# Transposes of q and k by DMA, and the four products with v of a pair of heads in one go, in an attention and MLP kernel

## The chip, the cores and the metric

The kernel runs on one core of one Trainium2 chip. The metric is the time of one execution on the device in microseconds (us). Three runs of the kernel before gave a median of 1263.84 us (1262.47 to 1264.2). All durations below come from one more execution, which the hardware profiler recorded.

## What is computed

```python
# q, k, v: (8 batches, 12 heads, 448 rows, 64); w_in 768x2048; w_out 2048x768
scores = q @ k.transpose(0, 1, 3, 2) / sqrt(64) - log(448)
attn = 1 / (1 + exp(-scores))          # a sigmoid, no softmax
x = (attn @ v).transpose(0, 2, 1, 3).reshape(8 * 448, 768)
h = x @ w_in
out = (h - tanh(h)) @ w_out
```

## The kernel before

**Numbers in two halves.** From batch 2 on, a float32 matrix is kept as two float16 parts, a high half and a low half (what the high half leaves over), after it was multiplied by a power of two, and a product is three float16 matmuls: high by high, high by low, low by high. Batch 0 multiplies float32 throughout its attention; batch 1 has its scores in halves and its products with v in float32.

**The engines.** TensorE (PE) multiplies into PSUM; ScalarE (ACT) and VectorE (DVE) read PSUM and SBUF; GpSimd (POOL) only adds squares; SyncE (SP) issues the DMAs, in order. The order of PE, ACT, DVE and POOL is the order in which the program records its instructions; SP's order is left to the scheduler.

**A batch.** `moe1` (line 663) multiplies x by w_in, 288 matmuls with no attention between them; ACT and DVE make `h - tanh(h)` of it (`mix`, line 740) and split it into halves. `moe2` (line 772) multiplies by w_out: 48 steps of six matmuls (`po`) for three full row tiles, then 16 steps for the remaining 64 rows (`por`), which count half. Between these steps `second` (line 939) runs blocks of the attention of the *next* batch, at the steps listed in `BLOCKS` (8, 12, ... 52).

**A block.** `stream` (line 429) yields them. A pair of heads, g, has four chunks of 112 rows of k and so two blocks, i = 0 and i = 1, of two chunks each. In program order a block records:

- transposes on PE: k of pair g+2 if i = 1 (with a small matmul behind it in the same PSUM tile, which spreads the sums of squares for the scales, line 316), q of pair g+1 if i = 0. Four transposes of 112x128 each (line 299) fill a PSUM tile with the tag `tr`, of which there is one;
- the scores of the two chunks (line 362: 12 matmuls, `sc`), each chunk's sigmoid on ACT (line 371, `a`);
- between the two sigmoids, the halves K of pair g+2 or Q of pair g+1 (`parts`, line 332): high half on ACT (Q) or DVE (K), low half on DVE (line 340);
- `do_av`: the products with v (line 386, `acc`, 12 matmuls) of the two chunks of the *block before*; after the fourth chunk ACT evacuates x and squares it;
- the halves of v of pair g+1 (i = 0, line 348), the halves of this block's weights (`ahl`, lines 377 and 378), the loads of pair g+3 (i = 0) or the norms of pair g+3 on ACT (i = 1, line 308).

Temporary tiles of `mix`, the sigmoids and `ahl` share eight buffers (`TP`). K and Q have two buffers each.

**The end of a batch.** The block at index `ALONE` of `BLOCKS` finishes the batch's last products with v; three steps later `batch_scales` (line 608) takes the largest sum of squares and makes the halves `xhl` (lines 625 and 626) for the next `moe1`, in three portions, two steps apart. The blocks behind it already belong to the batch after. The first blocks of all run in the first batch, in `moe1_32` and `first`, beside the conversion of w_out.

Of the kernel before, what the change touches and what calls it, by code (L numbers as in the profile page):

```python
# [8 lines left out]
F16 = mybir.dt.float16  # L9
BF16 = mybir.dt.bfloat16  # L10
F32 = mybir.dt.float32
# [3 lines left out]
AF = mybir.ActivationFunctionType  # L15
ALU = mybir.AluOpType
# [3 lines left out]
P = 128  # L20
D = 64
CK = 112
# [12 lines left out]
class Builder:  # L35
# [6 lines left out]

    BLOCKS = (8, 12, 16, 20, 24, 28, 32, 36, 40, 44, 48, 52)
    TAIL = (1, 2, 3, 4, 5)
    ALONE = 8
    BLOCKS0 = (2, 5, 8, 12, 16, 20, 24, 31, 38)
    BLOCKS1 = (4, 7, 10, 13, 16, 19, 22, 25, 28, 32, 36, 40, 44, 48, 52)

    TP = 8
    SHIFT = 4  # L50

    def __init__(self, ctx, tc, q, k, v, w_in, w_out, out):
        self.tc, self.nc = tc, tc.nc
# [29 lines left out]
        self.wo = self.wp.tile([P, self.NF * 2 + self.SHIFT, 2, self.HALF], F16, name="wo")  # L83

    def warm(self, n):

# [25 lines left out]

    def where(self, kind, r, i=0):

        t, n, m = (self.wi, self.NB, 256) if kind == "in" else (self.wo, 1, self.HALF)
        f = t.rearrange("p a b c -> p (a b c)").bitcast(F32)
        r = r * n + i * self.NF + self.SHIFT
        return f[:, r * m : (r + n) * m]

    def conv_load(self, p):  # L120
# [88 lines left out]

    def split(self, t, n, S, act):  # L210

        F = t[:, n + self.SHIFT].rearrange("p b c -> p (b c)").bitcast(F32)
# [81 lines left out]
    def transpose(self, n, name, tag="tr", bufs=1, t=None):  # L294
        nc = self.nc
        if t is None:
            t = self.ps.tile([P, 512], F32, name=name, tag=tag, bufs=bufs)
        for c in range(4):
            nc.tensor.transpose(t[:, c * CK : (c + 1) * CK], n[:, c].rearrange("p h d -> p (h d)"), self.ident[:CK, :CK])  # L299
        return t[:, : self.S]  # L300
# [7 lines left out]
            self.nc.scalar.activation(junk, t.rearrange("p a b d -> p (a b d)"), AF.Square, accum_out=ss[:, i : i + 1])  # L308
        return ss[:, :n]

    def scales(self, ss, pb):

        nc = self.nc
        n = ss.shape[1]
        pb = pb[:, self.S : self.S + n]
        nc.tensor.matmul(pb, self.onesf[:CK, :], ss, start=True, stop=True)
        t = self.sm.tile([P, 3], F32, name="tn")
        nc.scalar.activation(t[:, :n], pb, AF.Relu, bias=self.tiny, scale=2.1)
        y = self.pow2(t[:, :n], n, "n")
        i = self.sm.tile([P, 3], F32, name="in")  # L320
        nc.vector.tensor_scalar(i[:, :n], y, 2.0**49, None, op0=ALU.mult)
        s = self.sm.tile([P, 3], F32, name="sn", bufs=3)
        nc.vector.reciprocal(s[:, :n], i[:, :n])
        r = self.sm.tile([P, 2], F32, name="rn", bufs=5)
        nc.vector.scalar_tensor_tensor(
            r[:, 0:1], i[:, 0:1], 1.0 / math.sqrt(D), i[:, 1:2], op0=ALU.mult, op1=ALU.mult
        )
        if n == 3:
            nc.vector.tensor_scalar(r[:, 1:2], y[:, 2:3], 2.0**49 / A_SCALE, None, op0=ALU.mult)
        return s, r  # L330

    def parts(self, t, s, name, act):

        nc = self.nc
        o = self.qk.tile([P, 2, self.S], F16, name=name, tag=name)
        if act:
            nc.scalar.activation(o[:, 0], t, AF.Copy, scale=s)  # L337
        else:
            nc.vector.tensor_scalar(o[:, 0], t, s, None, op0=ALU.mult)
        nc.vector.scalar_tensor_tensor(o[:, 1], t, s, o[:, 0], op0=ALU.mult, op1=ALU.subtract)  # L340
        return o

    def prep_v(self, vn, s):
# [85 lines left out]
    def stream(self):  # L429
# [5 lines left out]
        G = (self.B - 1) * NP  # L435
        at = lambda g: (1 + g // NP, g % NP)
        splits = lambda g: at(g)[0] >= self.AV32
        qk, v, ss, sc, K, Q, vv = {}, {}, {}, {}, {}, {}, {}
# [8 lines left out]
            if g < G:  # L447
                ss[g] = self.norms(qk[g] + ([v[g]] if splits(g) else []))

        def turn(g, n, name):  # L450
            return self.transpose(qk[g][n], name) if g < G else None

        def turn_k(g):
            if g >= G:
                return None
            t = self.ps.tile([P, 512], F32, name="kT", tag="tr", bufs=1)
            turned = self.transpose(qk[g][0], "kT", t=t)
            sc[g] = self.scales(ss.pop(g), t)
            return turned

        def parts_k(g, t):
            if g < G:
                K[g] = self.parts(t, sc[g][0][:, 0:1], "K", not splits(g) and g not in (2, 3))

        def parts_q(g, t):
            if g < G:
                Q[g] = self.parts(t, sc[g][0][:, 1:2], "Q", True)
                qk.pop(g)

        def prep_v(g):  # L470
# [11 lines left out]
        norms(1)  # L482
        yield 0, False
        for g in range(2):
            parts_k(g, turn_k(g))
            yield 450, False
            parts_q(g, turn(g, 1, "qT"))
            load(g + 2)
            yield 450, False
        norms(2)  # L490
# [16 lines left out]

        for g in range(G):
            for i in range(2):
                if i:  # L510
                    t = turn_k(g + 2)
                elif g:
                    t = turn(g + 1, 1, "qT")
                pss = [self.scores(c, K[g], Q[g]) for c in (2 * i, 2 * i + 1)]
                aa = [self.weigh(pss[0], sc[g][1][:CK, 0:1])]
                if i:
                    parts_k(g + 2, t)
                elif g:
                    parts_q(g + 1, t)
                aa.append(self.weigh(pss[1], sc[g][1][:CK, 0:1]))  # L520
                do_av()
                if i == 0:
                    if g == 0:
                        prep_v(0)
                    prep_v(g + 1)
                if splits(g):
                    aa = [self.split_a(a) for a in aa]
                todo.extend((g, 2 * i + n, a) for n, a in enumerate(aa))
                if g and i == 0:
                    load(g + 3)  # L530
                elif g:
                    norms(g + 3)
                yield 2750, True
# [350 lines left out]
    def first(self, rest):  # L884
# [33 lines left out]
    def batch(self, b):  # L918
# [70 lines left out]
```

## Time and profile before

| | us |
|---|---|
| median of three runs | 1263.84 |
| the profiled execution's own time | 1264.8 |
| its span, first to last instruction | 1262.5 |
| PE busy | 1235.0 |
| DVE busy | 946.7 |
| ACT busy | 940.2 |
| POOL busy | 38.6 |

In a profile "busy" is time with an instruction in work; matmuls follow one another in a pipeline, so a group's busy time divided by its count is less than the mean duration of one. A wait is put down to the instruction that came last before the waiting one could go. "Landing" is the time from the issue of a DMA to its completion. A tile's name stands without its buffer number.

### The profile page before, as it was taken

To read this page: it belongs to the slowest core of one execution; us is meant where nothing else is said; L and a number is where in the kernel's file an instruction comes from. 1 tells how busy PE (TensorE), PEld (TensorE's weight loads), DVE (VectorE), ACT (ScalarE), POOL (GpSimd) and SP (SyncE) were. 2 spreads that over 40 slices of the span, in tenths; PEclk is the share of its full clock that TensorE was granted. 3 is DMA by queue.
4 is the path that set the end of the run, shared out by engine and by line. 5 is a ranking of instruction groups with operands and counts; after the bars stand their busy time and mean duration, and the time that the engine had idled before them with its cause. 6 is when DMAs were issued, how large, how long until landed. Compare 5 with 4: busy or idle time off the path is not lost.

```text
span 1262.5 us, 20449 instructions
## 1 busy us (share of the span) xinstructions
PE 1235.0 (98%) x8011; PEld 685.3 (54%) x8011; DVE 946.7 (75%) x1473; ACT 940.2 (74%) x1325; POOL 38.6 (3%) x38
## 2 busy tenths in 40 slices
PE   9889889999999999999999999999999999999998
PEld 3245445555556555665555655555556655555555
DVE  5989988789876797676965798667976769645930
ACT  6957788958998688886878688886888868753820
POOL 0100000000010000100000000000000000000000
PEclk9999999999999999999999999999999999999999
DMA  9943254100122101220022200221012200100001
GB/s 261 299 126 90 56 162 136 49 20 1 36 73 57 42 2 42 65 65 7 1 58 64 56 1 16 64 58 41 1 43 67 62 7 1 28 14 20 1 13 32
DMA packets 114367, 70.52 MB, mean 56 GB/s; under 512 B 91872, under 2 KB 104416, under 8 KB 114272
## 3 DMA queue, kind: packets, MB, share of 16 engines
q1 hardware_dynamic: 113344, 69.00, 20.6%
q8 instruction: 63, 1.03, 0.3%
q10 hardware_dynamic: 928, 0.23, 0.1%
q14 instruction: 32, 0.26, 0.1%
HBM read 58.20 MB, written 11.01 MB: 55 GB/s over the span
## 4 chain that ended last, share of the span: by engine, by line
PE 74%; DVE 14%; ACT 6%; issue 3%; DMA 3%; SPq 0%; DVEq 0%; ACTq 0%
PE ph L676 30%; PE po L798 25%; PE sc L362 6%; PE acc L386 5%; PE por L836 3%; DVE ahl L378 2%; ACT a L371 2%; DVE xhl L626 2%; DMA raw<-moe_w_in 1%; PE acc L396 1%; PE qT L299 1%; DVE xhl L625 1%; ACT wo L214 1%; DVE stb L151 1%; DVE m L750 1%
## 5 line engine op out<-in xcount | busy, mean ns | idle before, releaser
L798 PE MATMUL po<-wo,g 128*128 128x384 f16 x2304 | 391.4, 326 | 1.0 <-ACT o L827 1.0
L676 PE MATMUL ph<-xhl,wi 128*128 128x448 f16 x2016 | 382.6, 352 | 0.0
L798 PEld LDWEIGHTS <-g 128*128 128x128 f16 x2304 | 219.5, 98 | 171.3 <-issue 30.4
L676 PEld LDWEIGHTS <-wi 128*128 128x128 f16 x2016 | 196.7, 98 | 185.0 <-issue 1.8
L371 ACT ACTIVATE a<-sc,nls,rn 112x896 f32<-112x896 f32 x168 | 179.9, 1095 | 45.4 <-PE sc L362 38.3
L378 DVE SCALAR_TENSOR_TENSOR ahl<-a,ahl 112x896 f16<-112x896 f32 x144 | 155.7, 1122 | 58.6 <-ACT ahl L377 57.9
L746 ACT ACTIVATE u<-ph,ih 128x896 f32<-128x896 f32 x64 | 64.4, 1006 | 98.9 <-PE ph L676 95.3
L377 ACT ACTIVATE ahl<-a 112x896 f16<-112x896 f32 x144 | 128.0, 939 | 0.0
L362 PE MATMUL sc<-Q,K 64*112 64x448 f16 x1008 | 116.1, 362 | 3.8 <-ACT a L371 2.8
L750 DVE SCALAR_TENSOR_TENSOR m<-ph,ihk,u 128x896 f32<-128x896 f32 x64 | 73.5, 1148 | 54.9 <-ACT th L748 54.6
L386 PE MATMUL acc<-ahl,vhl 112*64 112x448 f16 x864 | 96.4, 357 | 0.5
L660 ACT ACTIVATE g<-m,Sg 128x896 f16<-128x896 f32 x64 | 66.6, 1041 | 34.1 <-DVE m L764 28.7
L764 DVE COPY_PREDICATED m<-u,th 128x896 f32<-128x896 uint32 x64 | 77.3, 1207 | 6.9 <-DVE m L761 0.5
L661 DVE SCALAR_TENSOR_TENSOR g<-m,Sg,g 128x896 f16<-128x896 f32 x64 | 73.4, 1147 | 8.8 <-ACT g L660 8.8
L340 DVE SCALAR_TENSOR_TENSOR Q<-qT,sn,Q 128x448 f16<-128x448 f32 x42 | 28.6, 682 | 67.9 <-ACT Q L337 67.9
L362 PEld LDWEIGHTS <-K 64*112 64x112 f16 x1008 | 60.6, 128 | 32.5 <-issue 6.8
L761 DVE SCALAR_TENSOR_TENSOR m<-q,m 128x896 f32<-128x896 f32 x64 | 69.9, 1093 | 8.3 <-ACT q L760 0.9
L706 PE MATMUL ph<-x,wi 128*128 128x448 f32 x192 | 74.8, 539 | 0.0
L751 DVE SCALAR_TENSOR_TENSOR th<-ph,ih,th 128x896 f32<-128x896 f32 x64 | 73.3, 1145 | 0.0
L763 ACT ACTIVATE u<-u,b 128x896 f32<-128x896 f32 x64 | 66.7, 1043 | 5.6 <-DVE m L750 3.6
L757 DVE SCALAR_TENSOR_TENSOR m<-q,m 128x896 f32<-128x896 f32 x64 | 69.5, 1087 | 0.0
L386 PEld LDWEIGHTS <-vhl 112*64 112x64 f16 x864 | 43.5, 109 | 47.8 <-issue 26.1
(134 smaller groups left out, 1323.0 us busy)
## 6 DMA issues: line engine op xcount, KB each, us to landing
raw<-moe_w_in SPq DMA_DIRECT2D x24, 512.0 KB, 7.5
rawo<-moe_w_out SPq DMA_DIRECT2D x32, 384.0 KB, 3.9
kn<-k SPq DMA_DIRECT2D x96, 112.0 KB, 2.9
vn<-v SPq DMA_DIRECT2D x48, 224.0 KB, 2.7
qn<-q SPq DMA_DIRECT2D x94, 112.0 KB, 2.9
out<-o SPq DMA_DIRECT2D x7, 336.0 KB, 3.1
out<-o SPq DMA_DIRECT2D x7, 288.0 KB, 3.1
out<-o SPq DMA_DIRECT2D x7, 240.0 KB, 2.6
```

The source lines that it names most:

```text
L362: nc.tensor.matmul(ps[:CK, h, :S], K[r, w, cs], Q[r, x, :], start=(n == 0), stop=(n == len(prods) - 1))
L371: nc.scalar.activation(a, ps[:CK, :, :S], AF.Sigmoid, bias=self.nls[:CK], scale=scale)
L377: nc.scalar.activation(A[:, 0], a, AF.Copy, scale=A_SCALE)
L378: nc.vector.scalar_tensor_tensor(A[:, 1], a, A_SCALE, A[:, 0], op0=ALU.mult, op1=ALU.subtract)
L386: nc.tensor.matmul(acc[h * D : (h + 1) * D, : self.S], v[:, w, h, c, :], A[:, x, h], start=(c == 0 and n == 0), stop=(c == 3 and n == 2),)
L661: nc.vector.scalar_tensor_tensor(g[:, 1], m, Sg, g[:, 0], op0=ALU.mult, op1=ALU.subtract)
L676: nc.tensor.matmul(ph[:, e, :S], self.wi[:, c * self.NB + k, part, e * P : (e + 1) * P], xhl[c][:, x, :], start=(i == 0), stop=(i == 3 * s ...
L706: nc.tensor.matmul(ph[:, e, :S], self.where("in", c)[:, f * P : (f + 1) * P], xs[c], start=(c == 0), stop=(c == self.NC - 1),)
L750: V.scalar_tensor_tensor(m, ps, ihk, u, op0=ALU.mult, op1=ALU.mult)
L751: V.scalar_tensor_tensor(th, ps, ih, th, op0=ALU.mult, op1=ALU.subtract)
L764: V.copy_predicated(m, u.bitcast(U32), th)
L798: nc.tensor.matmul(po[i][:, :H], gs[f // 2][:, x, f % 2, tk * P : (tk + 1) * P], self.wo[:, i * self.NF + f, w], start=(f == 0 and n == 0) ...
```

## The change

- Transposes of k and q for batches 1 to 7 leave PE. `parts` now scales and halves the tile as it was loaded (112 x 512, in SBUF) into a staging tile `w` (one buffer, both halves), and one `dma_start_transpose` on SP's queue turns both halves into K or Q. High half and low half are on the engines they were on. The small matmul for the scales gets a PSUM tile of its own under the tag `tr`. Batch 0 keeps its transposes on PE.
- From batch 2 on, `do_av` is left out of the blocks with i = 1, so that the next pair's block with i = 0 does four chunks in one go (24 matmuls).
- `ALONE` is 9 instead of 8: the batch's last products with v fall to the block at step 44, not 40, and three blocks of the batch after follow, not four. Batch 1's list has one block fewer, and batch 6's runs one more.
- One spare slot of w_out's tile is dropped (`SHIFT_O`), which makes room for `w`.

```diff
-    ALONE = 8
+    ALONE = 9
-    BLOCKS1 = (4, 7, 10, 13, 16, 19, 22, 25, 28, 32, 36, 40, 44, 48, 52)
+    BLOCKS1 = (4, 7, 10, 13, 16, 20, 24, 28, 32, 36, 40, 44, 48, 52)
...
+    SHIFT_O = 3
...
-    def parts(self, t, s, name, act):
+    def parts(self, n, s, name, act):
         nc = self.nc
+        flat = n.rearrange("p c h d -> p (c h d)")
+        w = self.qk.tile([CK, 2, 4 * P], F16, name="w", tag="w", bufs=1)
+        if act:
+            nc.scalar.activation(w[:, 0], flat, AF.Copy, scale=s[:CK])
+        else:
+            nc.vector.tensor_scalar(w[:, 0], flat, s[:CK], None, op0=ALU.mult)
+        nc.vector.scalar_tensor_tensor(w[:, 1], flat, s[:CK], w[:, 0], op0=ALU.mult, op1=ALU.subtract)
         o = self.qk.tile([P, 2, self.S], F16, name=name, tag=name)
-        if act:
-            nc.scalar.activation(o[:, 0], t, AF.Copy, scale=s)
-        else:
-            nc.vector.tensor_scalar(o[:, 0], t, s, None, op0=ALU.mult)
-        nc.vector.scalar_tensor_tensor(o[:, 1], t, s, o[:, 0], op0=ALU.mult, op1=ALU.subtract)
+        nc.sync.dma_start_transpose(
+            o.rearrange("p x (c t) -> p (x c) t", c=4), w.rearrange("p x e -> p (x e)")
+        )
         return o
...
         for g in range(G):
             for i in range(2):
                 if i:
-                    t = turn_k(g + 2)
-                elif g:
-                    t = turn(g + 1, 1, "qT")
+                    scales(g + 2)
                 pss = [self.scores(c, K[g], Q[g]) for c in (2 * i, 2 * i + 1)]
...
-                do_av()
+                if i == 0 or not splits(g):
+                    do_av()
```

On PE, at the start of a block with i = 1 in the steady state, before (kT is the transposed k, onesf and ss the small matmul's inputs, po the second product):

```order
L798 MATMUL po_4884<-wo,g 128x384
L299 MATMUL kT<-ident,kn 128x112 x4
L316 MATMUL kT<-ss,onesf 128x3
L362 LDWEIGHTS K
L362 MATMUL sc<-Q,K 112x448
```

and after:

```order
L796 MATMUL po_3752<-wo,g 128x384
L316 MATMUL pbn<-ss,onesf 128x3
L367 LDWEIGHTS K
L367 MATMUL sc<-Q,K 112x448
L367 LDWEIGHTS K
```

The four transposes are gone, and the small matmul has a tile of its own. At the end of the same block's scores, before:

```order
L362 MATMUL sc<-Q,K 112x448
L386 LDWEIGHTS vhl
L386 MATMUL acc<-ahl,vhl 64x448
L386 LDWEIGHTS vhl
L386 MATMUL acc<-ahl,vhl 64x448
```

and after:

```order
L367 MATMUL sc<-Q,K 112x448
L796 LDWEIGHTS g
L796 MATMUL po_3751<-wo,g 128x384
L796 LDWEIGHTS g
L796 MATMUL po_3752<-wo,g 128x384
```

The products with v that followed the scores have moved to the next block, behind its own scores.

More of the change, by code (lines that the diff above doesn't have):

```diff
@@ L82, in __init__ @@
         self.wi = self.wp.tile([P, self.NC * self.NB + self.SHIFT, 2, 256], F16, name="wi")
-        self.wo = self.wp.tile([P, self.NF * 2 + self.SHIFT, 2, self.HALF], F16, name="wo")
+        self.wo = self.wp.tile([P, self.NF * 2 + self.SHIFT_O, 2, self.HALF], F16, name="wo")
     def warm(self, n):
@@ L113, in where @@
     def where(self, kind, r, i=0):
-        t, n, m = (self.wi, self.NB, 256) if kind == "in" else (self.wo, 1, self.HALF)
+        t, n, m, shift = (self.wi, self.NB, 256, self.SHIFT) if kind == "in" else (self.wo, 1, self.HALF, self.SHIFT_O)
         f = t.rearrange("p a b c -> p (a b c)").bitcast(F32)
-        r = r * n + i * self.NF + self.SHIFT
+        r = r * n + i * self.NF + shift
         return f[:, r * m : (r + n) * m]
@@ L210, in split @@
     def split(self, t, n, S, act):
-        F = t[:, n + self.SHIFT].rearrange("p b c -> p (b c)").bitcast(F32)
+        F = t[:, n + (self.SHIFT if t is self.wi else self.SHIFT_O)].rearrange("p b c -> p (b c)").bitcast(F32)
         if act:
@@ L292, in load_v, with transpose @@
         return t
-    def transpose(self, n, name, tag="tr", bufs=1, t=None):
+    def transpose(self, n, name, tag="tr", bufs=1):
         nc = self.nc
-        if t is None:
-            t = self.ps.tile([P, 512], F32, name=name, tag=tag, bufs=bufs)
+        t = self.ps.tile([P, 512], F32, name=name, tag=tag, bufs=bufs)
         for c in range(4):
@@ L309, in norms, with scales @@
         return ss[:, :n]
-    def scales(self, ss, pb):
+    def scales(self, ss):
         nc = self.nc
         n = ss.shape[1]
-        pb = pb[:, self.S : self.S + n]
+        pb = self.ps.tile([P, 512], F32, name="pbn", tag="tr", bufs=1)[:, :n]
         nc.tensor.matmul(pb, self.onesf[:CK, :], ss, start=True, stop=True)
@@ L448, in norms, with scales, parts_k, parts_q @@
                 ss[g] = self.norms(qk[g] + ([v[g]] if splits(g) else []))
[L450 to L461, printed above, removed]
+        def scales(g):
             if g < G:
-                K[g] = self.parts(t, sc[g][0][:, 0:1], "K", not splits(g) and g not in (2, 3))
-        def parts_q(g, t):
+                sc[g] = self.scales(ss.pop(g))
+        def parts_k(g):
             if g < G:
-                Q[g] = self.parts(t, sc[g][0][:, 1:2], "Q", True)
+                K[g] = self.parts(qk[g][0], sc[g][0][:, 0:1], "K", not splits(g) and g not in (2, 3))
+        def parts_q(g):
+            if g < G:
+                Q[g] = self.parts(qk[g][1], sc[g][0][:, 1:2], "Q", True)
                 qk.pop(g)
```

9 lines of the change are left out of this document (5 added, 4 removed).

## The prediction

> **What bounds the kernel now.** I read the busy times of the whole span first, then one period of the steady state, then who TensorE (PE) waited for, then the time line of one pair of heads.
>
> ```profile
> PE 1235.0 (98%) x8011; PEld 685.3 (54%) x8011; DVE 946.7 (75%) x1473; ACT 940.2 (74%) x1325; POOL 38.6 (3%) x38
> ```
>
> PE is busy 98% of the 1262.5 us span. An average can hide stages, so the next view takes the stretch from one first product (moe1) to the next, in the steady state.
>
> ```profile
> core 0: us, PE busy (x) PEld busy (x) DVE busy (x) ACT busy (x) POOL busy (x), PEclk, DMA share, GB/s
> 423.50:570.50 147.00, 146.89 (x1026) 84.58 (x1022) 111.54 (x165) 116.13 (x159) 4.56 (x4) 1.00 0.15 39
> ```
>
> The columns are the length, then busy time (instructions) of PE, weight loads, DVE, ACT and POOL, then the granted clock, the DMA share and GB/s. In 147.0 us PE is idle 0.11 us. DVE (111.5) and ACT (116.1) have a quarter of the period free. Who ended PE's idle time from 266 to 1190 us:
>
> ```profile
> PE qT L299 <- ACT sqn L308: 1.0, 1, 1.0
> PE por L836 <- ACT o L827: 0.5, 1, 0.5
> ```
>
> 1.5 us in 924. So in the steady state the kernel is as long as PE's list of instructions: what is taken off that list comes off the time, one to one, until something else is late. Now two blocks of the attention (one pair of heads) inside the second product (time of start, length, engine, instruction):
>
> ```profile
> 674.87 0.55 PE L299 MATMUL qT<-ident,qn 112*128 112x112 f32 x4
> ...
> 675.35 1.34 PE L362 MATMUL sc<-Q,K 64*112 64x448 f16 x12
> ...
> 676.62 1.33 PE L386 MATMUL acc<-ahl,vhl 112*64 112x448 f16 x12
> 677.17 0.63 ACT L337 ACTIVATE Q<-qT,sn 128x448 f16<-128x448 f32 x1
> ...
> 677.83 0.68 DVE L340 SCALAR_TENSOR_TENSOR Q<-qT,sn,Q 128x448 f16<-128x448 f32 x1 [2.14 <-ACT Q L337]
> ...
> 677.88 4.07 PE L798 MATMUL po<-wo,g 128*128 128x384 f16 x24
> ...
> 681.79 0.55 PE L299 MATMUL kT<-ident,kn 112*128 112x112 f32 x4
> ...
> 682.18 0.30 PE L316 MATMUL kT<-ss,onesf 112*128 112x3 f32 x2
> ...
> 682.40 1.34 PE L362 MATMUL sc<-Q,K 64*112 64x448 f16 x12
> ...
> 683.79 0.68 DVE L339 TENSOR_SCALAR K<-kT,sn 128x448 f16<-128x448 f32 x1
> 684.51 0.68 DVE L340 SCALAR_TENSOR_TENSOR K<-kT,sn,K 128x448 f16<-128x448 f32 x1
> ...
> 686.18 2.09 DVE L378 SCALAR_TENSOR_TENSOR ahl<-a,ahl 112x896 f16<-112x896 f32 x2 [0.99 <-ACT ahl L377]
> ```
>
> A block is scores (sc, 12 matmuls: 676.62 − 675.35 = 1.27 us), products with v (acc, 12: 677.88 − 676.62 = 1.26 us) and 24 matmuls of the second product (681.79 − 677.88 = 3.91 us). Ahead of them stand the transposes, which this change takes off PE.
>
> **The transposes off PE.** From the first transpose of q to the first score is 675.35 − 674.87 = 0.48 us; from the first transpose of k to the small matmul of the norms (which stays) 682.18 − 681.79 = 0.39 us. Per pair 0.87 us; there are 42 pairs (seven batches of six): 42 × 0.87 = 36.5 us. The groups of the whole run bound it from above:
>
> ```profile
> L299 PE MATMUL qT<-ident,qn 112*128 112x112 f32 x168 | 23.6, 263 | 4.0 <-DVE K L340 2.7 <-ACT sqn L308 1.0 <-issue 0.3
> L299 PE MATMUL kT<-ident,kn 112*128 112x112 f32 x168 | 23.5, 262 | 2.3 <-DVE Q L340 2.3
> ```
>
> Their busy time is 23.6 + 23.5 = 47.1 us, 0.56 us for a group of four; that counts the overlap with the matmuls around them. I take 36.5, because the distances between starts are what the next matmul really waited, and keep 47.1 as the upper end. On PE the rest only changes places, the 12 acc matmuls of the odd block going behind the 12 of the even one: the same count at the same 0.105 us each, so nothing.
>
> Ahead of batch 2 PE also waited for the one PSUM buffer in which both transposes stood:
>
> ```profile
> PE qT L299 <- DVE K L340: 2.7, 2, 2.2
> PE kT L299 <- DVE Q L340: 2.3, 3, 1.0
> ```
>
> Us in total, times, longest: together 5.0 us. The buffer stays for the small matmul only, so these waits go. What is late next there is DVE, which converts w_out and is busy 65.55 of 70 us in that stretch (columns as above):
>
> ```profile
> 90.00:160.00 70.00, 64.77 (x212) 33.69 (x213) 65.55 (x110) 52.87 (x75) 0.00 (x0) 0.97 0.25 67
> ```
>
> So I credit 3 of the 5.0 us (0 to 5).
>
> **The work on DVE and ACT.** Scaling and halving now read 112×512 float32 from SBUF instead of 128×448 from PSUM. The same shapes stand in the trace as the work on v and the squares:
>
> ```profile
> L349 DVE SCALAR_TENSOR_TENSOR vhl<-vn,sn,vhl 112x512 f16<-112x512 f32 x36 | 27.1, 752 | 1.3
> ...
> L308 ACT ACTIVATE sqn<-kn 112x512 bf16<-112x512 f32 x42 | 26.1, 621 | 0.0
> ...
> L348 DVE TENSOR_SCALAR vhl<-vn,sn 112x512 f16<-112x512 f32 x36 | 17.2, 477 | 0.0
> ```
>
> DVE per pair: K's high half 0.68 → 0.48, two low halves 0.68 → 0.75 each, together 2.04 → 1.98 us. ACT: Q's high half 0.63 → 0.62. Nothing either way.
>
> **The new transfers.** Each pair issues two DMA transposes on SP's queue, 112 × 2 × 512 × 2 bytes = 224 KB each. The trace of before has none, so their time from issue to landing, t, is bounded by its transfers (KB, median us to landing):
>
> ```profile
> raw<-moe_w_in SPq DMA_DIRECT2D x24, 512.0 KB, 7.5
> ...
> kn<-k SPq DMA_DIRECT2D x96, 112.0 KB, 2.9
> vn<-v SPq DMA_DIRECT2D x48, 224.0 KB, 2.7
> ```
>
> The same 224 KB land in 2.7 us as a plain load (vn); the longest median of the page is 7.5 us (raw). I take 3.5, nearer to the load of equal size, some more because each 2-byte element changes its place. What hides it: K is made three blocks and Q two blocks ahead of the scores that read it, so PE's own deadline is 13 us away. The nearer deadline is the staging tile w, of which there is one: the next high half cannot be written before the transfer has read the last one. By the time line: Q's low half ends at 677.83 + 0.68 = 678.51, and K's high half starts at 683.79, 5.3 us later; K's ends at 685.19 and the next Q's starts at 691.14 (the rows below), 5.9 us later, which becomes some 4.5 since the odd block loses its 1.26 us of acc and a transpose. As one loop, a pair needs 2t plus the four instructions between (0.62 + 0.75 + 0.48 + 0.75 = 2.6) plus some 0.3 of gaps, 2t + 2.9, in a pair's period of 13.98 − 0.87 = 13.1 us (675.35 to 689.33 before). It fits while t is under 5.1 us; at 3.5 it takes 9.9. On SP the Q transpose stands ahead of the q and v loads of a pair three ahead, and K's ahead of the k loads; those loads wait for the same low half anyway, to have their buffer free, so what they lose is one issue. Cost: none, if t stays under 5.1.
>
> The Trainium skill speaks to t twice. DMA: Bandwidth & Descriptors, "Latency and other measured facts", gives 261 GB/s for a transpose with a non-contiguous middle dimension, by which the 224 KB move in an estimated 0.9 us, and the sum stands. VectorE: DVE Perf Modes, "The three transpose paths", gives 1309 ns for one 128×128 block by DMA, and its rules send a 128×128 transpose to TensorE when PSUM will do; eight such blocks one after another would be an estimated 10.5 us, and the sum fails (the slower rival below). No run shown here has a transpose by DMA. In the 17% of that rival 7 are for this rule.
>
> On SP, at the end of a batch's second product, before (kn, qn, vn: loads of k, q, v; out: stores):
>
> ```order
> L285 DMA kn<-k 112x4x64 x2
> L790 DMA out<-orem 64x384 x2
> L285 DMA qn<-q 112x4x64 x2
> L291 DMA vn<-v 112x2x256
> L285 DMA kn<-k 112x4x64 x2
> ```
>
> and after, at the same place:
>
> ```order
> L343 DMA_TRANSPOSE K<-w 128x8x112
> L286 DMA kn<-k 112x4x64 x2
> L343 DMA_TRANSPOSE Q<-w 128x8x112
> L286 DMA qn<-q 112x4x64 x2
> L292 DMA vn<-v 112x2x256
> L788 DMA out<-orem 64x384 x2
> L343 DMA_TRANSPOSE K<-w 128x8x112
> ```
>
> The two transposes of each pair have come in between its loads; no more than two loads or stores and one v load stand ahead of either, so no long queue.
>
> **Four chunks together.** The odd block has no acc now. The even block's third chunk needs the odd block's halves of the weights (ahl), which ended at 686.18 + 2.09 = 688.27, that is 5.9 us after the odd block's first score (682.40). PE gets there after 1.27 + 3.91 + 1.27 + 2 × 0.63 = 7.7 us. Slack 1.8 us: no wait, unless ACT or DVE is held up by more than that.
>
> **One block less ahead.** The sum of the squares, and with it the halves of x (xhl), move one block later in a batch. Before:
>
> ```profile
> 689.33 1.34 PE L362 MATMUL sc<-Q,K 64*112 64x448 f16 x12
> ...
> 691.14 0.63 ACT L337 ACTIVATE Q<-qT,sn 128x448 f16<-128x448 f32 x1
> ...
> 696.83 0.62 DVE L605 TENSOR_REDUCE m<-nm 128x1 f32<-128x448 f32 x1
> ...
> 708.16 0.69 DVE L626 SCALAR_TENSOR_TENSOR xhl<-x,Sx,xhl 128x448 f16<-128x448 f32 x1
> ...
> 717.69 4.52 PE L676 MATMUL ph<-xhl,wi 128*128 128x448 f16 x23
> ```
>
> From the block's first score (689.33) to the last half of x (708.16 + 0.69) is 19.5 us, and to the next moe1 (717.69) 28.4 us. One block later leaves 28.4 − 7.0 and less two transposes: some 20.5 us. The evacuation of acc now waits for 1.26 us more of acc, so the halves are ready 19.5 to 21 us after. moe1 uses the last of the six halves only after 15 of its matmuls, 15 × 0.19 = 2.8 us in (4.52 us for 23 of them in the last row). So it just fits: 0 to 1 us for a batch, six batches, and I put 1 us on the sum. The block taken from the second product of batch 1 comes back in that of batch 6: no change.
>
> **The sum.** 1264.8 (the profiled execution's own time; 2.3 us of it lie outside the span) − 36.5 − 3 + 1 = 1226.3. The profiled run lies 1.0 us above the median of the runs shown (1263.84), so I predict 1225.
>
> **The rivals.**
> *Slower: transfers longer than PE's period.* If t is over 5.1 us, the loop through w sets the pair's period: 2t + 2.9. Break-even is where 36 pairs (batches 2 to 7) lose the 39.5 us gained: 13.1 + 1.1 = 2t + 2.9, t = 5.65. At the 7.5 us of the slowest row the period is 17.9 us: 36 × 4.8 = 173 us, so 1225 + 173 ≈ 1398. Transposes that go block after block, eight to a transfer, would be the mechanism. For it: only one w, nothing in the trace shows the transfer, and PE has no slack to give. Against it: the same bytes land in 2.7 us, and the DMA engines are 15% busy in the steady period. 17%.
> *Half the gain: ACT late.*
>
> ```profile
> 633.00:717.00 84.00, 83.89 (x681) 51.22 (x681) 59.34 (x108) 69.82 (x111) 4.55 (x4) 1.00 0.25 65
> ```
>
> ACT is busy 69.8 us in the 84 of a second product with its blocks; 12 × 0.435 us less leave 78.8 us, 89%. With t near 5 ACT stands before w, then its halves of the weights come more than the 1.8 us late, and PE waits ahead of the third chunk. Half a pair's gain lost, 42 × 0.43 = 18 us: 1243. 12%.
> *More: the whole busy time.* 47.1 + 5 us off, 1264.8 − 52 − 1 = 1212. Against it speak the distances of starts. 7%.
> *Nothing:* t near the break-even of 5.65, the gain paid back: 1263. 4%.
>
> **The numbers.** The forecast itself, with 1218 to 1232 as its own range, has 60%. A measurement of this kernel tells some 0.2% (2.5 us) from no change. Faster: 60 + 12 + 7 = 79%; within: 4%; slower: 17%. The range runs from the upper bound of the saving, 1212, to 1262, which leaves out the slower case and little else.
>
> **What would show it.** The period from moe1 to moe1 should fall from 147.0 to 147.0 − 6 × 0.87 = 141.8 us, PE stay idle under 1 us in it, and the landing of K and Q stand under 5 us. I am wrong if PE's waits in the steady state name K, Q or ahl; if ACT or DVE wait for a transfer before writing w; or if moe1 waits for xhl.

## The result, and the profile after

The kernel after takes 1244.99 us (median of four runs, 1241.85 to 1250.16); the kernel before took 1263.15 us beside it. The ratio is 0.9852 [0.9828, 0.9877]: faster by 18.2 us, where 38.5 were predicted. The profiled execution of after took 1250.16 us (span 1247.9), the slowest of its four; where two profiles are subtracted below, this is kept apart.

The page of after, its busy times and the landing times of its transposes (from issue to completion, us, in the last column):

```profile
PE 1202.3 (96%) x7675; PEld 651.9 (52%) x7675; DVE 941.6 (75%) x1473; ACT 942.0 (75%) x1325; POOL 38.0 (3%) x38
...
K<-w SPq DMA_TRANSPOSE x42, 3.0
Q<-w SPq DMA_TRANSPOSE x42, 2.9
```

PE's work fell by 1235.0 − 1202.3 = 32.7 us, its share of the span from 98 to 96%: part of the work that left PE came back as waiting. The transposes land in 3.0 us (3.5 was the guess), under the 5.1 us from which they would bind. One period of the steady state, the columns as in the prediction:

```profile
427.76:569.59 141.83, 141.24 (x976) 79.20 (x976) 110.92 (x166) 116.14 (x160) 4.56 (x4) 1.00 0.26 59
```

141.83 us, PE idle 0.59: what the prediction asked for (141.8, under 1 us). So the steady state came out as told in this period, and most of the loss is elsewhere. The chain of waits shows where: the first products (moe1) of the batches, before (start in us, length, engine, tile, line):

```profile
266.18 47.79 PE ph L676 x252
423.71 54.59 PE ph L676 x288
...
1146.72 54.59 PE ph L676 x288
```

and after:

```profile
276.07 54.60 PE ph L674 x288
427.76 54.60 PE ph L674 x288
...
1132.05 54.59 PE ph L674 x288
```

From the second batch's first product to the last one's it went from 880.54 to 855.98 us, 24.6 us less. But that first one came 9.9 us *later*, with 16 groups of transposes off PE ahead of it. One more mark divides that: the small matmul `pb`, which ends the loading of w_in (the last two numbers are the first and last start of the two), before

```profile
L250 PE MATMUL pb<-mx,onesf x2: 245/256/266, 85.3 to 85.5; 1*128 1x1 f32 x2
```

and after:

```profile
L251 PE MATMUL pb<-mx,onesf x2: 245/256/266, 90.7 to 90.9; 1*128 1x1 f32 x2
```

| stretch | before | after | difference | predicted |
|---|---|---|---|---|
| start to pb | 85.5 | 90.9 | +5.4 | 0 |
| pb to the first moe1 | 180.7 | 185.2 | +4.5 | −10 |
| that moe1 to the last | 880.5 | 856.0 | −24.6 | −28.6 |
| last moe1 to the end | 115.8 | 115.8 | 0 | 0 |

(Predicted: 8 pairs × 0.87 and the 3 us of waits in the second row, 34 × 0.87 less 1 in the third.) The spans differ by 14.6 us. The first row is probably not the change's: no transpose, product or halving that it moves runs before 104 us (it also shifts the place of tiles in SBUF). The windows of that stretch, before

```profile
0.00:85.00 85.00, 75.67 (x332) 26.75 (x332) 65.02 (x119) 61.33 (x92) 6.11 (x10) 1.00 0.94 247
```

and after

```profile
0.00:85.00 85.00, 73.73 (x319) 25.31 (x320) 59.54 (x109) 56.81 (x87) 6.16 (x10) 0.98 0.95 238
```

show full DMA queues in both (0.94, 0.95) and 247 against 238 GB/s. Two kernels below whose instructions on PE, DVE, ACT and SP are the same up to 115 us differ in the same way. So the likely reading is that this stage varies from execution to execution and that the profiled run of after caught a long one.

The second row is the question: 14.5 us of the missing gain. The windows from pb to the first moe1, before and after:

```profile
85.50:266.18 180.68, 170.56 (x908) 90.96 (x909) 160.15 (x317) 142.84 (x249) 5.13 (x4) 0.97 0.32 91
90.90:276.07 185.17, 165.39 (x844) 85.51 (x845) 159.85 (x316) 143.34 (x248) 4.56 (x4) 0.97 0.44 108
```

PE's work fell by 5.2 us there, and its idle time rose from 10.1 to 19.8 us. The mean granted clock is 0.97 in both, so it is not the clock that makes the difference. PE's waits between 160 and 262 us (us in total, times, longest), after:

```profile
PE sc L367 <- ACT a L376: 7.3, 5, 2.5
PE wl L178 <- DVE stb L152: 4.1, 4, 1.4
PE wl L178 <- DMA rawo<-moe_w_out: 2.2, 1, 2.2
```

Before, PE waited there for the transposes' PSUM buffer (2.3 + 2.2 us). Those waits went, as predicted, and others came: PE waits for sigmoids, and for the conversion of w_out (wl, stb, rawo). ScalarE in turn waits for w_out's loads, which it did for 0.8 us before:

```profile
ACT stb L146 <- DMA rawo<-moe_w_out: 7.0, 2, 6.0
```

SP's time line there, after, shows those loads (rawo) behind transposes:

```profile
201.32 2.46 SPq L343 DMA_TRANSPOSE Q<-w  x1
203.82 1.25 SPq L286 DMA_DIRECT2D qn<-q  x2
205.17 1.98 SPq L131 DMA_DIRECT2D rawo<-moe_w_out  x4
...
213.60 1.27 SPq L343 DMA_TRANSPOSE K<-w  x1
214.98 0.51 SPq L131 DMA_DIRECT2D rawo<-moe_w_out  x1
```

A transpose mostly takes 1.25 us to issue (these columns are start and length), and its queue stands until VectorE has written the low half. In the kernel before the last load of w_out was issued at 202.4 us, here at 215.0, which is 7 us later when both are counted from pb.

### The profile page after: what moved, and what is told of

It reads as the page before. It is cut to its first block, busy times and chain, and to the rows that moved or that the text cites. A ratio compares the mean times of both kernels' runs of the same rounds, so it can differ in the third digit from the quotient of the medians.

```text
span 1247.9 us, 19830 instructions
## 1 busy us (share of the span) xinstructions
PE 1202.3 (96%) x7675; PEld 651.9 (52%) x7675; DVE 941.6 (75%) x1473; ACT 942.0 (75%) x1325; POOL 38.0 (3%) x38
## 2 busy tenths in 40 slices
DMA packets 192317, 89.76 MB, mean 72 GB/s; under 512 B 169824, under 2 KB 182368, under 8 KB 192224
## 3 DMA queue, kind: packets, MB, share of 16 engines
q1 hardware_dynamic: 191296, 88.28, 30.4%
## 4 chain that ended last, share of the span: by engine, by line
PE 71%; DVE 11%; ACT 10%; DMA 4%; issue 3%; SPq 1%; DVEq 0%; ACTq 0%
PE ph L674 31%; PE po L796 22%; PE sc L367 6%; PE acc L391 5%; PE por L834 5%; DMA raw<-moe_w_in 2%; ACT a L376 2%; ACT ahl L382 1%; ACT sqn L308 1%; DVE ahl L383 1%; DVE m L748 1%; DVE m L762 1%; DVE m L759 1%; DVE g L659 1%; DMA K<-w 1%
## 5 line engine op out<-in xcount | busy, mean ns | idle before, releaser
L796 PEld LDWEIGHTS <-g 128*128 128x128 f16 x2304 | 220.1, 98 | 183.5 <-issue 43.4
L376 ACT ACTIVATE a<-sc,nls,rn 112x896 f32<-112x896 f32 x168 | 179.5, 1092 | 18.7 <-PE sc L367 18.2
L658 ACT ACTIVATE g<-m,Sg 128x896 f16<-128x896 f32 x64 | 66.7, 1042 | 32.7 <-DVE m L762 27.3
L391 PE MATMUL acc<-ahl,vhl 112*64 112x448 f16 x864 | 89.0, 355 | 0.8 <-DVE ahl L383 0.8
L341 DVE SCALAR_TENSOR_TENSOR w<-qn,sn,w 112x512 f16<-112x512 f32 x42 | 31.5, 750 | 70.5 <-ACT w L338 70.2
L391 PEld LDWEIGHTS <-vhl 112*64 112x64 f16 x864 | 46.0, 110 | 40.6 <-issue 13.4
```

Source lines behind the costliest of these rows:

```text
L376: nc.scalar.activation(a, ps[:CK, :, :S], AF.Sigmoid, bias=self.nls[:CK], scale=scale)
L391: nc.tensor.matmul(acc[h * D : (h + 1) * D, : self.S], v[:, w, h, c, :], A[:, x, h], start=(c == 0 and n == 0), stop=(c == 3 and n == 2),)
L796: nc.tensor.matmul(po[i][:, :H], gs[f // 2][:, x, f % 2, tk * P : (tk + 1) * P], self.wo[:, i * self.NF + f, w], start=(f == 0 and n == 0) ...
```

## The experiments

Three theories of the start: **A**, w_out's loads are held up in SP's queue by the transposes. **B**, the start was never PE's: VectorE and ScalarE set its length, so taking work off PE gives nothing there, and late data only costs. **D**, K and Q themselves come later by the detour through w and the transfer. Beside them stands the question what grouping the products is worth; where an expectation names another theory, it says itself what that is. Ratios are against the kernel before, run on the same chip.

**The first eight pairs' transposes back on PE**, all else as after:

```diff
+    ON_PE = 8
...
-        def scales(g):
+        def turn_k(g):
+            if g < self.ON_PE:
+                t = self.ps.tile([P, 512], F32, name="kT", tag="tr", bufs=1)
+                T["K"] = self.transpose(qk[g][0], "kT", t=t)
+                sc[g] = self.scales(ss.pop(g), t[:, self.S :])
...
-                K[g] = self.parts(qk[g][0], sc[g][0][:, 0:1], "K", ...)
+                f, t = (self.parts_pe, T["K"]) if g < self.ON_PE else (self.parts, qk[g][0])
+                K[g] = f(t, sc[g][0][:, 0:1], "K", ...)
```

> The changed kernel, with the transposes of k and q of the first eight pairs (all that are made before the second batch's first product) on PE again; the same numbers are computed. Theory A (in the first batch the DMA transposes stand on SP's queue ahead of w_out's loads, and hold them up until DVE has written w): the first batch takes as long as before, some 266 us to the second first product, and the rest keeps its gain of 24 us, so 1238 to 1240 us, 5 to 6 faster than the changed kernel, although 16 groups of transposes (7 us) are back on PE. Theory B (the first batch is bound by DVE and ACT, and w_out's loads have nothing to do with it): 1238 to 1246, PE's waits for the converted w_out stay at some 8 us. Theory C (the loss is only spread between runs, slower loads in batch 0): 7 us slower than the changed kernel.

Measured: 1238.03 us (1237.02 to 1239.06), ratio 0.9792 [0.9777, 0.9807]: 7 us faster than after, though PE does 16 groups of transposes more. Its chain has the first moe1 at

```profile
264.91 54.60 PE ph L704 x288
```

with pb at 83.7, so 181.2 us from pb (before 180.7, after 185.2), and 855.0 us from there to the last moe1 (after 856.0). The waits for the PSUM buffer are back, and ScalarE's for w_out's loads are down to 0.8 us, as before:

```profile
PE qT L301 <- DVE K L360: 2.7, 2, 2.2
...
PE kT L301 <- DVE Q L360: 2.0, 3, 0.9
```

So the loss of this stretch lies with the first eight pairs: with their transposes on PE, and the waits for the buffer with them, it is as long as before.

**w_out's loads issued by POOL instead of SP:**

```diff
-        self.nc.sync.dma_start(p["raw"], src[...])
+        queue = self.nc.gpsimd if kind == "out" else self.nc.sync
+        queue.dma_start(p["raw"], src[...])
```

> The changed kernel, with the 32 loads of w_out issued from POOL's queue, so that no load of w_out stands behind a transpose. Theory A (SP's queue holds up the loads): PE's waits for the converted w_out (10.6 us by line wl) fall under 4 us and the second first product starts 8 to 14 us earlier, 1231 to 1237 us. Theory B (DVE and ACT bound the first batch): within 3 us of the changed kernel, 1242 to 1248. If POOL's own issue of a load is slow or held up by its sums of squares, later loads and a slower first batch.

Measured: 1246.48 us (1245.5 to 1249.33), ratio 0.9856 [0.984, 0.9873], no change. It decides nothing: five of the loads stood behind one of POOL's own sums of squares, so ScalarE's wait for rawo stayed (7.4 us), and PE waited 3.7 us for a transposed Q. The same with batch 1's sums of squares on VectorE:

```diff
-            nc.gpsimd.tensor_tensor(out, self.x2, x2, op=ALU.add)
+            adds = nc.gpsimd if self.split_done else nc.vector
+            adds.tensor_tensor(out, self.x2, x2, op=ALU.add)
```

> The kernel after with w_out's raw loads issued by GpSimd instead of SyncE, and batch 1's sums of squares added on VectorE, so that nothing else stands in GpSimd's queue until the first product of batch 1. Theory A (what the first pairs lose is that w_out's loads stand in SyncE's queue behind transposes that wait for VectorE): the waits of ScalarE and TensorE for raw w_out (7.0 and 2.2 us) go and the first product of batch 1's neighbourhood comes some 8 us earlier: 1236 to 1240. Theory B (the start is bound by VectorE and ScalarE's conversion work, and the late loads only show where that lies): 1244 to 1249, up to 3 us slower for the additions on VectorE.

Measured: 1248.74 us (1247.9 to 1252.89), ratio 0.9887 [0.9858, 0.9916]. Nothing is gained, so A by itself is not borne out: with w_out's loads out of SP's queue ScalarE's wait for them shrinks from 7.0 to 2.9 us (two times), and yet pb to the first moe1 takes 186.3 us (after 185.2). It is no clean test, because the landing of other transfers changed too in this stretch, 160 to 230 us:

```profile
qn<-q SPq DMA_DIRECT2D x8, 112.0 KB, 5.0
...
Q<-w SPq DMA_TRANSPOSE x4, 5.4
```

In after q's loads landed in 3.0 us there and Q's transposes in 3.6. The loads of k and v became faster instead, from 4.1 to 2.7 and from 4.9 to 3.3 us, and PE waited 1.5 us for a transposed Q. Why the one group became slower and the other faster is not shown.

**Less work for PE in the start, with no transfer for it.** As the first experiment, but one of the four transposes of each group; K and Q of these pairs read its 112 columns four times, so their attention is computed from one chunk of k and q:

```diff
-        for c in range(4):
+        for c in range(1 if name in ("kT", "qT") else 4):
...
+        if name in ("kT", "qT"):
+            return t[:, None, :CK].to_broadcast([P, 4, CK])
```

> The first eight pairs' transposes on TensorE as in the first experiment, but one of the four of each group only; K and Q read its 112 columns four times, so the attention of those pairs is computed from one chunk of k and q instead of four. It takes 16 groups x some 0.33 us = 5 us of matmuls out of the start without any transfer in their place. The prediction's step (each transposed group is worth 0.39 to 0.48 us of the time wherever it stands): 1238 - 5 = 1233, first product at 260. Theory B (up to the first product the start is as long as VectorE's and ScalarE's work, whatever TensorE has to do): within 1 us of the first experiment, 1237 to 1239, first product at 264 to 265.

Measured: 1238.57 us (1237.78 to 1240.1), ratio 0.9797 [0.9777, 0.9818], the same as with all transposes. The windows from pb to the first moe1 say why; the first experiment, then this one:

```profile
83.70:264.91 181.21, 170.89 (x908) 91.10 (x909) 159.92 (x317) 143.10 (x249) 4.69 (x4) 0.97 0.32 90
84.10:264.64 180.54, 165.27 (x860) 85.99 (x861) 159.61 (x316) 142.12 (x249) 4.83 (x4) 0.98 0.32 91
```

PE has 5.6 us less to do, and the stretch is 0.7 us shorter: the rest became idle time, 15.3 us instead of 10.3. PE just waits longer for the PSUM buffer, 6.4 us instead of 4.2 between 160 and 262 us (4.2 behind Q's low half and 2.2 behind K's, against 2.0 and 2.2). This part of B is shown: there, taking transposes off PE gains next to nothing. That VectorE sets the stretch, busy for 160 us of it, or VectorE and ScalarE (143) by turns, is argued from these figures; no run makes their work less.

**Both: K and Q from PE, and the transfers too.** As the first experiment; in addition the halves of K and Q are transposed by DMA into w as soon as VectorE has written the low half, and nobody reads the result. They take 112 of the 128 rows, 7/8 of the bytes of the change's own transfers:

```diff
+        w = self.qk.tile([P, 8 * P], F16, name="w", tag="w", bufs=1)
+        nc.sync.dma_start_transpose(
+            w[:, : 7 * CK].rearrange("p (c t) -> p c t", c=7), o.rearrange("p x e -> p (x e)")[:CK]
+        )
```

> The first experiment's kernel (first eight pairs' K and Q made from TensorE's transposes, 1238.0) with 16 transfers added whose result nobody reads: as soon as VectorE has written the low half of K or Q of those pairs, the tile is transposed by DMA into the staging tile (7/8 of the bytes of the change's own transfer), on SyncE's queue, at the places where the kernel after has its own. Theory A (the start loses by what the transposes do to SyncE's in-order queue and to the DMA engines): most of the 7 us come back, first product at 270 or later, 1243 to 1246. Theory D (it loses because K and Q come later, after staging and transfer, and k's and q's buffers are held longer; the queue doesn't matter): first product at 265, 1237 to 1239.

Measured: 1239.9 us (1239.07 to 1242.48), ratio 0.9799 [0.9778, 0.9819]: 1.9 us over the first experiment, with overlapping intervals. ScalarE's wait for w_out's loads is back in its profile, as long as in after, and yet little is lost:

```profile
ACT stb L147 <- DMA rawo<-moe_w_out: 6.3, 3, 3.6
```

From pb (87.5) to the first moe1 (271.01) it takes 183.5 us: 2.3 more than in the first experiment (181.2), 1.7 less than after (185.2). Both differences are larger than the scatter: the kernels here with these pairs' transposes all on PE and no such transfers take 180.0 to 181.2 us (before, the first experiment, twelve pairs, grouping alone, and the three blocks pulled ahead), and those with all by DMA and w_out's loads on SP's queue 185.2 to 186.4 (after, no grouping, blocks moved). So the transfers on the queue cost some 2 us. That the other 1.7 us go with the detour of K and Q is a subtraction, not a measurement. It also bears on the first row of the table: up to 115 us its instructions are the first experiment's, in the same order, but the first 85 us ran at 242 GB/s here

```profile
0.00:85.00 85.00, 74.83 (x326) 26.02 (x327) 63.11 (x116) 59.22 (x91) 6.29 (x10) 0.98 0.96 242
```

and at 254 there, with pb at 87.5 and 83.7. So the same instructions can differ by 3.8 us in that stage. Chance is not the only reading, though: of the seven profiles in which some of the first eight pairs go through DMA transposes, five have pb at 87.1 us or later (the others at 83.7 and 84.4), and the six without have it at 83.7 to 85.7. How transfers that come later could act on that stage is not seen in the profiles.

**Four and twelve pairs on PE** (ON_PE = 4 and 12):

```diff
-    ON_PE = 8
+    ON_PE = 4
```

> As the first experiment, but the transposes of only the first four pairs on TensorE (pairs 4 to 7 by DMA). The first two pairs' stand beside the conversion before the first blocks, pairs 2 to 5 beside the loads of w_out, pairs 6 and 7 behind them. If the loss comes where w_out is loaded, pairs 4 and 5 bring part of it back: 1240 to 1243. If it all comes with the first pairs, 1237 to 1238 (or 1 us less, for pairs 6 and 7).

> As the first experiment, but the transposes of the first twelve pairs on TensorE (batch 1, and batch 2 but for two pairs of the next). By the periods (146.3 with grouping alone, 141.8 with the transposes by DMA too) a pair's transposes are worth 0.75 us in the steady state: 1238.0 + 4 x 0.75 = 1241. By the prediction's 0.87: 1241.5. If the gain of the steady state were the grouping's alone: 1238.

Measured: four, 1241.76 us (1241.71 to 1244.82), ratio 0.9822 [0.9801, 0.9842]; twelve, 1239.19 (1237.98 to 1241.04), 0.9797 [0.9777, 0.9817]. With four, pb to moe1 takes 183.5 us: about half of the 4.0 us between the first experiment (181.2) and after (185.2) comes with pairs 4 to 7, beside w_out's loads. With twelve it stays at 181.0, and the next stretch grows. The chain of waits of twelve:

```profile
264.67 54.60 PE ph L704 x288
418.73 54.60 PE ph L704 x288
```

It is 154.06 us, against 416.82 − 264.91 = 151.91 with eight: 2.15 us for four pairs, 0.54 each, less than the 0.75 expected. But a lower clock in the stretch with eight hides part of it. The same 23 matmuls of the second product, in the first experiment and in the kernel with both:

```profile
351.02 5.58 PE L826 MATMUL po<-wo,g 128*128 128x384 f16 x23 [1.28 <-DVE o L856]
```

```profile
357.10 3.90 PE L830 MATMUL po<-wo,g 128*128 128x384 f16 x23 [1.28 <-DVE o L860]
```

The granted clock was 0.70 in the first and 1.00 in the second. The kernel with both runs the same instructions in this stretch, in 421.23 − 271.01 = 150.22 us. Against that, twelve pairs on PE cost 3.84 us, 0.96 a pair. So 0.75 lies between the two readings; the medians differ by 1.2 us for the four, which the intervals do not tell from none.

**The change without the grouping** (do_av in every block, ALONE and batch 1's list as before):

```diff
-                if i == 0 or not splits(g):
-                    do_av()
+                do_av()
```

> The changed kernel without its second and third part: products with v in every block, four blocks ahead, the lists of before; the transposes stay on the DMA. If the waits of the second product for the evacuation of its PSUM buffers (po behind ACT and DVE, 7.2 us) come from the odd block, which has only 1.5 us of work now: those waits go, the steady period is 141.8 us or a little less in every batch, 1238 to 1241 us. If they come from ACT and DVE being later in general: no change beyond 2 us. If the grouping itself saved PE time: slower by more than 3 us.

Measured: 1251.7 us (1249.94 to 1252.49), ratio 0.9898 [0.9883, 0.9913], 6.7 us slower than after. PE waits where it did not, from 266 us on:

```profile
PE acc L391 <- DVE ahl L383: 4.3, 16, 0.6
PE sc L367 <- DVE m L602: 2.4, 5, 0.6
```

**The grouping alone**, with all transposes on PE (the kernel before with ALONE = 9, after's list for batch 1, and the same condition):

```diff
-                do_av()
+                if i == 0 or not splits(g):
+                    do_av()
```

> The kernel before with one part of the change alone: from batch 2 on the products with v of a pair's four chunks together (24 in a row) and the later end of a batch; all transposes stay on TensorE. The prediction's step: the products only change places, 12 at 0.105 us each, so nothing is gained, and 1 us is lost at the ends of batches: 1264 to 1265. Theory A, from the time line of the kernel after (24 products in a row take 2.39 us, two times 12 take 2 x 1.26 = 2.52): 0.13 us for each of 36 pairs, 4.7 us, less some 1 to 2 us of waits for the second product's evacuations: 1260 to 1261, with a period of some 146.4 us from first product to first product (147.0 before). Theory C: grouping was worth 6.7 us beside the DMA transposes because it also took away waits for the weights' halves (ahl); those waits are absent here, so 1257 would need another cause.

Measured: 1261.84 us (1260.23 to 1263.88), ratio 0.9984 [0.9973, 0.9995]: 2 us faster. The period is 146.31 us (713.58 to 859.89 in its chain), 147.0 before. A pair on PE's time line, with grouping alone:

```profile
643.95 1.34 PE L362 MATMUL sc<-Q,K 64*112 64x448 f16 x12
645.22 4.07 PE L799 MATMUL po<-wo,g 128*128 128x384 f16 x24
649.13 0.55 PE L299 MATMUL qT<-ident,qn 112*128 112x112 f32 x4
649.61 1.34 PE L362 MATMUL sc<-Q,K 64*112 64x448 f16 x12
650.88 2.46 PE L386 MATMUL acc<-ahl,vhl 112*64 112x448 f16 x24
653.28 4.07 PE L799 MATMUL po<-wo,g 128*128 128x384 f16 x24
...
657.80 1.34 PE L362 MATMUL sc<-Q,K 64*112 64x448 f16 x12
```

and in after, without the transposes:

```profile
658.91 1.34 PE L367 MATMUL sc<-Q,K 64*112 64x448 f16 x12
660.19 4.07 PE L796 MATMUL po<-wo,g 128*128 128x384 f16 x24
664.19 1.34 PE L367 MATMUL sc<-Q,K 64*112 64x448 f16 x12
665.46 2.46 PE L391 MATMUL acc<-ahl,vhl 112*64 112x448 f16 x24
667.86 4.07 PE L796 MATMUL po<-wo,g 128*128 128x384 f16 x24
...
671.98 1.34 PE L367 MATMUL sc<-Q,K 64*112 64x448 f16 x12
```

A pair is 13.98 us before, 657.80 − 643.95 = 13.85 with grouping, 671.98 − 658.91 = 13.07 with both. The 24 products in a row take 653.28 − 650.88 = 2.40 us, two times 12 took 2.52. The transposes are worth 0.78, not 0.87: the second product's 24 matmuls take 3.91 us up to a transpose (649.13 − 645.22) and 4.00 up to a score (664.19 − 660.19), so 0.09 us of what was counted as the transpose's start stays.

The four kernels, from the second batch's first moe1 to the last one's (by their chains):

| us | products by twos | by fours |
|---|---|---|
| transposes on PE | 880.5 (before) | 878.0 |
| by DMA (the first eight pairs too) | 862.9 | 856.0 (after) |

Grouping gives 2.5 us by itself and 6.9 beside the transposes by DMA; these give 17.6 and 22.0. Together they do more than their sum, since the shorter block brings the products with v to weights' halves that are not ready (ahl, 16 waits), and the grouping gives the halves a block's time more. The 856.0 of after also holds a stretch of low clock (0.71) behind the second batch's first product, where 23 matmuls take 5.37 us instead of 3.90; the other three have none there, so without it the numbers beside the DMA would be some 1.5 us larger (6.9 and 22.0).

**Two tries at the last waits of the steady state.** After waits for the evacuation of the second product's two PSUM buffers, which follows a row tile's end and is now covered by a block of 1.3 us (scores alone), from 266 us on:

```profile
PE po L796 <- DVE o L826: 4.9, 6, 1.3
PE po L796 <- ACT o L825: 2.3, 3, 1.3
```

First the blocks were moved so that longer blocks stand at the ends of row tiles:

```diff
-    BLOCKS = (8, 12, 16, 20, 24, 28, 32, 36, 40, 44, 48, 52)
+    BLOCKS = (6, 9, 12, 16, 20, 24, 28, 32, 36, 40, 44, 48)
```

> The changed kernel with the blocks of batches 2 to 6 at steps 6, 9, 12, 16, 20 to 48, so that the long even block and not the short odd one follows the end of a row tile (steps 16, 32, 48), where PE waits for the evacuation. If the short odd block uncovers the evacuation: the waits of po go in batches 2 to 6 (0.6 to 1.2 us each, 4 to 5 in all), 1240 us. If the earlier blocks at 6 and 9 collide with the tail of the first product on DVE and ACT: new waits there, equal or slower by 2 to 6 us.

Measured: 1248.03 us (1246.98 to 1251.03), ratio 0.9875 [0.9857, 0.9893]. The wait for VectorE's evacuation shrank, from 4.9 to 1.3 us, and one for the sigmoids came, from 266 us on:

```profile
PE sc L367 <- ACT a L376: 5.4, 10, 0.9
...
PE po L796 <- DVE o L826: 1.3, 1, 1.3
```

Then, on top of the first experiment, three blocks were pulled one step ahead (in batch 1's list likewise):

```diff
-    BLOCKS = (8, 12, 16, 20, 24, 28, 32, 36, 40, 44, 48, 52)
+    BLOCKS = (8, 11, 16, 20, 24, 27, 32, 36, 40, 43, 48, 52)
```

> The first eight pairs' transposes on TensorE as in the first experiment (1238.0), and the three blocks that stand just behind the end of a row tile (steps 12, 28 and 44; one without products with v) pulled one step ahead (11, 27, 43). Theory A: the waits of the second product for its two PSUM buffers' evacuation (po: 4.2 + 2.3 us) stem from a short block at that place and go: 1232 to 1234. Theory B: as when the blocks were shifted the other way, the wait only moves to the scores (for ScalarE's sigmoids): 1237 to 1241.

Measured: 1238.35 us (1236.52 to 1243.03), ratio 0.98 [0.9772, 0.9828], the same as the first experiment; the wait for VectorE's evacuation stayed at 4.2 us, ScalarE's went from 2.3 to 1.6. So pulling these blocks ahead does not remove that wait; what does, without bringing another as the first try did, was not found.

## Why the prediction was wrong

1244.99 us lies outside the forecast's own 1218 to 1232, though inside the wide range of 1212 to 1262, and the gain is less than half of the one forecast.

**The step that failed** is the count: "there are 42 pairs (seven batches of six): 42 × 0.87 = 36.5 us", with "So I credit 3 of the 5.0 us". It priced the first eight pairs, 16 of the 84 groups, at PE's price, though the prediction had shown the row of that stretch (VectorE 65.55 of 70 us) and used it for the waits alone. There PE's work was not the bound: 5.6 us less of it (one transpose of four) made the stretch 0.7 us shorter, and the rest came back as waits. Instead of −10 us the stretch from pb to the first moe1 took +4.5 us in the profiles. With these pairs on PE it is 4.0 us shorter: some 2.3 us are shown to come with transfers on SP's queue (those that nobody reads), and the rest is put down to the way of K and Q through w by subtraction. By the medians the kernel with these pairs on PE takes 1238.0 instead of 1245.0 us; what the 7.0 us hold beyond the 4.0 cannot be divided by stages, since the loading stage differs and each median has it in its own way.

**Transposes in the steady state: nearly right, by two errors.** It is 0.78 us a pair rather than 0.87, and the grouping, put at nothing ("the same count at the same 0.105 us each"), 0.13: together 0.91, less the new waits for evacuations, which gave nearly the predicted period (141.83 against 141.8). That the errors cancel is luck. From the first moe1 to the last the sum was 24.6 us instead of 28.6. Of the 4.0 missing 1.2 are a period of 142.98 us (711.42 to 854.40), in which one wait for an evacuation took 1.3 us, and some 1.5 are the stretch of low clock; the rest was not taken apart.

**What held.** The landing time: 3.0 us for 3.5, and the loop through w does not bind PE in the steady state. One sign that the prediction had named did show: from the second batch's first product on ScalarE waits for a transfer before writing w, twice and not for long, and no wait of PE names K or Q there:

```profile
ACT w L338 <- DMA K<-w: 3.2, 2, 2.5
```

The Trainium skill's 1309 ns for one 128×128 block by DMA (VectorE: DVE Perf Modes, "The three transpose paths"), taken eight times, gives an estimated 10.5 us for this transfer; the traces do not bear that out. The 261 GB/s of the Trainium skill's DMA: Bandwidth & Descriptors ("Latency and other measured facts"), an estimated 0.9 us for the bytes, is not contradicted: what was measured includes issue and completion. The work on VectorE and ScalarE stayed what it was (946.7 to 941.6 us, 940.2 to 942.0). Q's high half takes 0.72 us on ScalarE where 0.62 was expected. PE waits for ahl 0.8 us in all after the first moe1, so the four chunks together nearly fit; no first product waits for xhl, so one block less ahead fits.

**The rivals.** The slower one did not come: t is under 5.1. The time of "half the gain" (1243) is near the measured one, but not its mechanism, which was ScalarE standing before w in the steady state and PE waiting for it: PE idles 0.59 us in the period shown, and no wait of PE there comes from w. That the number is near is luck.

**Open** stay what sets the length of the start (VectorE, ScalarE or both), what exactly the detour costs there (the way through w, the later release of k's and q's buffers and the slower transfers were not taken apart), and what makes the first 85 us differ between the profiles.

## What to carry to other kernels

Before multiplying a gain per instance by the number of instances, divide them by stage, and ask for each stage which engine it waits for: here a fifth of the instances lay in a stage that PE's work did not set, and they cost time instead of giving it. The cure was to move work off an engine only where that engine is the bound, and to leave the old way in place elsewhere (1238.0 us; no kernel here has a lower median). Two edits that each change a block's length should be tried alone and together, since one may hide the wait that the other makes.

## What the runs showed of the hardware

A DMA transpose of 112 × 1024 two-byte elements from SBUF to SBUF landed in 2.9 to 3.0 us by the medians of after (2.9 to 4.8 over all 84), about as long as a plain load of the same 224 KB (3.1 us there). Four of Q's took 5.4 us (median) in the kernel with w_out's loads alone on POOL's queue; in the other kernel with these loads on POOL the same four took 3.0, so the loads beside them do not explain it by themselves. A transpose held SP's queue for 1.25 us at its issue, and behind it waited whatever came next. The kernel's packets went from 114367 to 192317, and queue q1's share of the DMA engines' time from 20.6 to 30.4% of the span, that is by an estimate (0.304 × 1247.9 − 0.206 × 1262.5) / 84 = 1.4 us of all 16 engines for each of the 84 transfers.

Matmuls of one kind in a row are cheaper than in two pieces: 24 products in 2.40 us, two times 12 in 2.52. And what stands behind a group changes what the group takes: 24 matmuls of the second product take 3.91 us up to a transpose and 4.00 us up to a score.

The granted clock was not the same for the same work: 23 matmuls of the second product took 5.58 us at a granted clock of 0.70 and 3.90 at 1.00, in two kernels with the same instructions there.
